# Attention scores as native float32 products of row halves, and another order of work in the staging of two weight matrices

## Chip, cores and metric

The kernel runs on one core of a Trainium2 chip. The metric is device microseconds of one execution, as the median of several runs.

## What is computed

Four batches of attention with 12 heads, 448 positions and head size 64, with a mix of the heads before and after the softmax; then two blocks of dense layers on the 1792 x 768 result. All inputs are float32, and the products keep about that precision.

```python
scores = scale * np.matmul(q, k.transpose(0, 1, 3, 2))
scores = np.einsum('bhij,hg->bgij', scores, w_pre)
attn = np.exp(scores - np.max(scores, axis=-1, keepdims=True))
attn = attn / (np.sum(attn, axis=-1, keepdims=True) + 1e-09)
attn = np.einsum('bhij,hg->bgij', attn, w_post)
x = np.matmul(attn, v)                     # to [1792, 768]
h = (x @ w1) * (x @ w2) @ w3
x = h @ w_out
h = np.maximum(x @ w_in, 0.0)
out = h * h @ w_out2
```

## The kernel before

Engines are named as the profile does: PE is TensorE, DVE VectorE, ACT ScalarE, POOL GpSimd, SP the queue that issues loads. Every engine runs its instructions in the order in which the program was written; that order is fixed by hand, by tables of steps.

**Staging of weights (class Weights, and Prod34, which uses it first).** Since `w3` and `w_out` are applied one after the other, the kernel first multiplies them with each other. A product of about float32 precision is made of three fast ones: each operand is split into a high part (rounded to the type float32r) and a low part (the difference), and `mm3` (L54) adds high x high, high x low and low x high. Weights arrive as 64-bit words, and a piece goes through: a load on SP (L69), `narrow` on ACT (L81), three joins of bits on DVE (L93, L95, L97) that give float32 `f`, `high` on ACT (L111), `rest`, the low part, on POOL (L115). `Prod34.half0` walks over 25 pieces: for each of eight chunks two of 384 columns (`wo`) and one of 512 (`w3`), and multiplies each chunk into eight accumulators, 24 products of 384 columns a chunk. `stage(s)` sets what is done ahead for later pieces: load 6 ahead, narrow 4, joins 3 and 2 (the joins of two pieces interleaved), high 2, rest 1. At its end ACT and DVE copy the accumulators out (L195, L196). `half1` does the same with eight more `w3` pieces: a loop over chunks with 12 products each, then four groups of 24 products.

**Prologue of attention.** `prologue(i)` is called after each chunk, with i from 0 to 7 in half0 and from 8 to 19 in half1. The table PRO says at which i the first chunk of queries (n = 0) is loaded, split and scored. From i = 15 on it also runs the first steps of attention.

**Attention.** Queries come in 16 chunks of 120 or 88 rows (four a batch), each cut into 12 or 9 blocks of up to 10 rows x 12 heads; there are 180 blocks g. Step g of `attention_step` issues for TensorE in this order: pv (L478, of an earlier chunk, in some steps), premix of block g + 1 (sp, L380), scores of a later chunk (sc, L358, in some steps), tmix of block g - 4 (tp, L436). Scores leave PSUM through ACT (`evac`, L365), are regrouped by a DMA (L372), mixed, and turned by rowmax (DVE), expo (ACT), a sum scaled on POOL, p_hi (ACT) and p_lo (DVE, L426) into half-precision high and low parts; after tmix, p2 (L449 on ACT, L451 on DVE) takes them out of PSUM.

**Scores before.** K has its 64 rows twice on the partitions of the loaded tile: rows 0 to 63 become the high part (a cast on ACT in the first batch, on DVE later: L312, L310), rows 64 to 127 the low part (L319). Q is doubled likewise and split into `qh` (L334, L336) and `ql` (L341). So one product over 128 rows gives q-part x (k high + k low), and a head is two products of 448 columns, `qh` and `ql`, into one of two PSUM banks. premix and pv use float32 operands as they are; the trace shows each such product as two records. pv writes its two heads to the PSUM partitions 0 to 63 and 64 to 127.

Of the kernel before, what the change touches and what calls it, by code (L numbers as in the profile page):

```python
# [34 lines left out]
def fused_kernel(ctx, tc, q, k, v, w_pre, w_post, w1, w2, w3t, wo, win, wo2, eye, out):  # L35
# [22 lines left out]
    class Weights:  # L58
# [60 lines left out]
    class Prod34:  # L119


        def __init__(self, p, stg, spare):
            self.p, self.stg, self.spare = p, stg, spare
            self.w = Weights(stg, PW, 5, 3, 4, 2, 2)
# [10 lines left out]
            for i in range(-6, 0):  # L135
                self.stage(i)

        def tile(self, k, c, x):
            if (k, c, x) not in self.t:
                n = HC if k == "o" else PW  # L140
                p = self.p if x else self.stg
                kw = {"tag": "w3{}", "bufs": 2} if (k, x) == ("3", 0) else {"tag": "w" + k + "{}" + f"{c}_{x}"}
                self.t[k, c, x] = tuple(
                    p.tile([128, n], R, name=f"w{k}{e}{c}_{x}", tag=kw["tag"].format(e), bufs=kw.get("bufs", 1))
                    for e in "hl"
                )
            return self.t[k, c, x]

        def stage(self, s):
            w = self.w  # L150
            ok = lambda i: 0 <= i < len(self.seq)
            if ok(s + 6):
                k, c, x, lo, hi, _ = self.seq[s + 6]
                src, n = (wo, HC) if k == "o" else (w3t, PW)
                w.load(s + 6, src[c, :, n * x + lo : n * x + hi], True)
            if ok(s + 4):
                w.narrow(s + 4)
            if ok(s + 2) and s > 0:
                w.join(s + 2, 1)
            if ok(s + 3):  # L160
                w.join(s + 3, 0)
                if s < 0:
                    w.join(s + 3, 1)
                    w.join(s + 3, 2)
            if ok(s + 2):
                if s >= 0:
                    if s == 0:
                        w.join(s + 2, 1)
                    w.join(s + 2, 2)
                k, c, x, lo, hi, _ = self.seq[s + 2]  # L170
                w.place(s + 2, tuple(t[:, lo:hi] for t in self.tile(k, c, x)))
                w.high(s + 2)
            if ok(s + 1):
                w.rest(s + 1)
# [6 lines left out]
        def half0(self, ps, between):  # L181
# [8 lines left out]
            for m in range(4):  # L190
                if m > 1:
                    self.stage(self.n0 - 2 + m)
                o = f32(self.spare.tile([128, 2, S], R, tag="kt", name=f"o34_{m}", bufs=8))
                o = o.rearrange("p e j -> p (e j)")[:, :DM]
# [6 lines left out]
        def store(self, m, h, acc):  # L201
            if m % 2 == 0:
                self.o = self.spare.tile([128, 3, 2, 128], F, tag="kraw", name=f"o34_{m}_{h}", bufs=2)
# [38 lines left out]
    class Attention:  # L242
        def __init__(self, const, ka, ps):
            self.const, self.ka, self.ps, self.sc = const, ka, ps, {}
            self.done = set()
            self.kt, self.kraw, self.qraw, self.qh, self.ql = {}, {}, {}, {}, {}
# [14 lines left out]
        def setup_load(self):  # L261
            nc.vector.memset(self.ones, 1.0)
            for x in self.phl:
                for t in x:
                    nc.vector.memset(t[:, S:], 0.0)
# [13 lines left out]
        def setup_post(self):  # L279
            kw, kab = (self.ka.tile([120, 12, 10], F, tag="qraw", name=x, bufs=2) for x in ("kw", "kab"))  # L280
# [17 lines left out]

        def load_k(self, b, r):
            if b == 0 and r in (2, 3):  # L300
                raw = f32(self.ka.tile([128, 2, S], R, tag="kt", name=f"kraw{b}_{r}", bufs=8))
            else:
                raw = self.ka.tile([128, 2, S], F, tag="kraw", name=f"kraw{b}_{r}", bufs=2)
            nc.sync.dma_start(raw, k[b, :, 2 * r : 2 * r + 2])
            self.kraw[b, r] = raw

        def high_k(self, b, r):
            t = self.ka.tile([128, 2, S], R, tag="kt", name=f"kt{b}_{r}", bufs=8)
            if b:
                nc.vector.tensor_copy(t, self.kraw[b, r])  # L310
            else:
                nc.scalar.activation(t, self.kraw[b, r], AF.Copy)  # L312
            self.kt[b, r] = t

        def low_k(self, b, r):
            raw, t = self.kraw.pop((b, r)), self.kt[b, r]
            for e in range(2):
                eng = nc.gpsimd if b else nc.vector
                eng.tensor_tensor(t[64:128, e], raw[64:128, e], f32(t[64:128, e]), ALU.subtract)  # L319
            self.done.add(("k", b, r))  # L320

        def load_q(self, n, g4):
            b, c = divmod(n, 4)
            i0, ic, _ = CHUNKS[c]
            o = 12 * i0 + 4 * g4 * ic
            raw = self.ka.tile([128, 4 * IC], F, tag="qraw", name=f"qraw{n}_{g4}", bufs=2)
            nc.sync.dma_start(raw[:, : 4 * ic], q[b, :, o : o + 4 * ic])
            self.qraw[n, g4] = raw[:, : 4 * ic]

        def high_q(self, n, g4):  # L330
            th = self.ka.tile([128, 4 * IC], R, tag="qh", name=f"qh{n}_{g4}", bufs=3)
            th = self.qh[n, g4] = th[:, : 4 * CHUNKS[n % 4][1]]
            if n:
                nc.vector.tensor_copy(th, self.qraw[n, g4])  # L334
            else:
                nc.scalar.activation(th, self.qraw[n, g4], AF.Copy)  # L336

        def low_q(self, n, g4):
            tl = self.ka.tile([128, 4 * IC], R, tag="ql", name=f"ql{n}_{g4}", bufs=3)
            tl = self.ql[n, g4] = tl[:, : 4 * CHUNKS[n % 4][1]]  # L340
            nc.gpsimd.tensor_tensor(tl, self.qraw.pop((n, g4)), f32(self.qh[n, g4]), ALU.subtract)  # L341

        def split_q(self, n, g4):
            self.high_q(n, g4)
            self.low_q(n, g4)

        def scores(self, n, h):
            b, c = divmod(n, 4)
            ic = CHUNKS[c][1]
            assert ("k", b, h // 2) in self.done  # L350
            if h == 0:
# [3 lines left out]
            sc = self.ps.tile([IC, S], F, tag="sc", name=f"sc{n}_{h}", bufs=2)  # L355
            g4, hh = divmod(h, 4)
# [4 lines left out]
            self.sc[n, h] = sc  # L361

        def evac(self, n, h):
            ic = CHUNKS[n % 4][1]
            nc.scalar.activation(self.st[n][:ic, h], self.sc.pop((n, h))[:ic], AF.Copy)  # L365
            self.done.add(("s", n, h))

        def regroup(self, g):
            n, r, nr, o, cnt = blocks[g]
            assert all(("s", n, h) in self.done for h in range(NH))  # L370
# [83 lines left out]
        def p2_act(self, g):  # L454
            if g % 4 == 0:
                self.p2_evac(g, 0)

        def p2_dve(self, g):
            if g % 4:
# [34 lines left out]
    def spread(lo, hi, items):  # L494
# [3 lines left out]
    AT = {"sc": 1, "lq": 6, "hq": 3, "pv": 5, "k": -9, "ks": 4, "v": -6}  # L498
# [6 lines left out]
        "load_q": (2, 4, 9), "split_q": (5, 8, 13), "load_k": (7, 7, 8, 8, 8, 8), "high_k": (8, 9, 9, 12, 12, 12),  # L505
        "low_k": (9, 10, 12, 13, 13, 13), "scores": (10, 11, 12, 13, 15, 14), "evac": (10, 11, 13, 14, 15, 14),
# [3 lines left out]
    def attention_plan():  # L510
# [5 lines left out]
        for n in range(16):  # L516
            b = n // 4
            if n:
                for t, h in spread(first[n - 1] - RG + AT["sc"], first[n] - RG - 1, range(NH)):
                    add(t, "scores", n, h)  # L520
# [389 lines left out]
```

## Time and profile before

| | us |
|---|---|
| median of 3 runs | 1403.97 (1403.86 to 1404.88) |
| the profiled execution | 1406.93 |
| its span, in which the rows are counted | 1405.1 |
| PE busy | 1360.5 (97%) |
| DVE busy | 919.4 (65%) |
| ACT busy | 714.0 (51%) |
| POOL busy | 413.5 (29%) |

The span has four parts: 0 to 66 us half0, 66 to 129.7 half1 with the first steps of attention, 129.7 to about 563 attention, and the dense layers to the end. A row of the timeline gives start, length and instruction; where PE's instructions overlap in its pipeline, the time of one is read from start to start. In the table of stages the figure behind the engines is the granted clock of PE as a share of 2.4 GHz.

### The profile page before, as it was taken

How to read it: one execution, taken by the hardware profiler on the slowest of the kernel's cores; microseconds unless marked ns; L12 is line 12 of the kernel's file. 1: busy time of each engine (PE TensorE's matmuls, PEld its weight loads, DVE VectorE, ACT ScalarE, POOL GpSimd, SP SyncE). 2: the span in 40 equal slices, each digit the busy share in tenths (PEclk: the TensorE clock that was granted, in tenths of full speed). 3: DMA queues.
4: the chain of work that ended last, by engine and by line, in shares of the span. 5: the costliest groups of instructions: out<-in, count | busy, mean ns of one | idle time of the engine just before them, and what ended most of it. 6: DMA issues, size and time to landing. Idle time of an engine off the chain costs nothing.

```text
span 1405.1 us, 24056 instructions
## 1 busy us (share of the span) xinstructions
PE 1360.5 (97%) x8858; PEld 1141.8 (81%) x8858; DVE 919.4 (65%) x1561; ACT 714.0 (51%) x1529; POOL 413.5 (29%) x424
## 2 busy tenths in 40 slices
PE   6779999999999998999999999999999999999998
PEld 5767666667667666899999999999999999999998
DVE  8963887886887779655217944985555128935962
ACT  4455887877777877434224533543343224533430
POOL 4531351351242113222222222233222222322231
PEclk9889999999999999999999999999999999999999
DMA  7754455454545335434123342455343123432341
GB/s 216 228 187 159 157 167 163 158 177 150 169 165 169 119 128 157 139 102 113 54 69 101 124 120 73 122 176 175 115 115 91 59 78 96 131 115 79 117 145 54
DMA packets 95514, 183.77 MB, mean 131 GB/s; under 512 B 20581, under 2 KB 62053, under 8 KB 94949
## 3 DMA queue, kind: packets, MB, share of 16 engines
q1 hardware_dynamic: 89861, 178.82, 41.2%
q10 hardware_dynamic: 5536, 3.42, 0.8%
q8 instruction: 70, 1.15, 0.4%
q14 instruction: 47, 0.39, 0.1%
HBM read 129.52 MB, written 14.16 MB: 102 GB/s over the span
## 4 chain that ended last, share of the span: by engine, by line
PE 89%; DVE 5%; ACT 2%; issue 2%; DMA 1%; POOL 1%; DVEq 0%; ACTq 0%; POOLq 0%
PE l L54 50%; PE sp L380 10%; PE y L54 8%; PE tp L436 7%; PE pv L478 6%; PE sc L358 5%; PE q L54 2%; DVE pl L426 1%; DVE f L93 1%; DVE f L95 1%; DVE f L97 1%; PE p L54 1%; DVE p L451 1%; PE e L54 1%; ACT ph L419 1%
## 5 line engine op out<-in xcount | busy, mean ns | idle before, releaser
L115 POOL TENSOR_TENSOR wl<-f,wh 128x384 fp32r<-128x384 f32 (+1 forms) x176 | 195.6, 1115 | 508.5 <-ACT wh L111 492.8
L93 DVE TENSOR_SCALAR f<-y 128x384 int32<-128x384 int32 (+2 forms) x209 | 146.9, 703 | 88.2 <-POOL wl L115 83.3
L426 DVE SCALAR_TENSOR_TENSOR pl<-p,sm,ph 120x448 f16<-120x448 f32 x180 | 138.9, 772 | 77.0 <-ACT ph L419 76.3
L380 PE MATMUL sp<-r,kpre 120*120 120x448 f32 x360 | 178.2, 577 | 1.2 <-ACT p L394 0.8
L436 PEld LDWEIGHTS <-ph 120*128 120x128 f16 (+1 forms) x1440 | 105.5, 98 | 52.6 <-issue 52.6
L97 DVE SCALAR_TENSOR_TENSOR f<-raw,f 128x384 int32<-128x384 int32 (+2 forms) x209 | 140.4, 672 | 6.1
L95 DVE SCALAR_TENSOR_TENSOR f<-y,f 128x384 int32<-128x384 int32 (+2 forms) x209 | 140.3, 672 | 6.1
L54 PE MATMUL l<-blh,wh 128*128 128x448 f32 x384 | 141.1, 368 | 0.0
L54 PE MATMUL l<-bhh,wl 128*128 128x448 f32 x384 | 141.1, 368 | 0.0
L54 PE MATMUL l<-bhh,wh 128*128 128x448 f32 x384 | 141.1, 368 | 0.0
L111 ACT ACTIVATE wh<-f 128x384 fp32r<-128x384 f32 (+1 forms) x176 | 96.5, 549 | 86.5 <-DVE f L97 80.9
L365 ACT ACTIVATE s<-sc 120x448 f32<-120x448 f32 (+1 forms) x192 | 99.2, 543 | 76.4 <-PE sc L358 73.0
L436 PE MATMUL tp<-kwh,ph 120*128 120x120 f16 x720 | 125.7, 219 | 1.1 <-DVE p L451 1.1
L394 ACT ACTIVATE p<-sp,nm 120x448 f32<-120x448 f32 x180 | 114.2, 635 | 23.4 <-DVE nm L386 21.9
L386 DVE TENSOR_REDUCE nm<-sp 120x1 f32<-120x448 f32 x180 | 110.6, 615 | 21.0 <-PE sp L380 19.8
L358 PE MATMUL sc<-kt,qh 128*120 128x448 f32 (+1 forms) x192 | 119.5, 622 | 5.0 <-DVE kt L319 4.6
L436 PE MATMUL tp<-kwh,pl 120*128 120x120 f16 x720 | 124.1, 216 | 0.0
L436 PE MATMUL tp<-kwl,ph 120*128 120x120 f16 x720 | 124.0, 216 | 0.0
L81 ACT ACTIVATE y<-raw 128x384 f32<-128x384 f32 (+2 forms) x209 | 120.6, 577 | 5.9 <-DMA raw<-w3t 3.8
L419 ACT ACTIVATE ph<-p,sm 120x448 f16<-120x448 f32 x180 | 119.9, 666 | 5.8 <-DVE sm L414 4.6
L478 PE MATMUL pv<-p,v 112*64 112x120 f32 (+1 forms) x1536 | 94.6, 266 | 6.5 <-DVE p L451 6.2
L409 POOL TENSOR_SCALAR sm<-sm 120x2 f32<-120x2 f32 (+3 forms) x94 | 25.9, 276 | 254.4 <-ACT p L394 226.5
(122 smaller groups left out, 3155.5 us busy)
## 6 DMA issues: line engine op xcount, KB each, us to landing
r<-s SPq DMA_DIRECT2D x172, 210.0 KB
raw<-w SPq DMA_DIRECT2D x64, 384.0 KB
raw<-win SPq DMA_DIRECT2D x64, 384.0 KB
raw<-wo SPq DMA_DIRECT2D x48, 512.0 KB
kraw<-k SPq DMA_DIRECT2D x24, 448.0 KB
qraw<-q SPq DMA_DIRECT2D x36, 240.0 KB
raw<-w3t SPq DMA_DIRECT2D x15, 512.0 KB
raw<-wo SPq DMA_DIRECT2D x16, 384.0 KB
```

The source lines that it names most:

```text
L54: nc.tensor.matmul(acc, w, x, start=(first and i == 0 and j == 0), stop=(last and i == n - 1 and j == 2))
L81: nc.scalar.activation(y, self.raw[i][:, :, 1].bitcast(F), AF.Copy, scale=2.0**-112)
L93: nc.vector.tensor_scalar(fi, yi, 3, 0x7FFFFFFF, ALU.logical_shift_left, ALU.bitwise_and)
L95: nc.vector.scalar_tensor_tensor(fi, yi, -0x80000000, fi, ALU.bitwise_and, ALU.bitwise_or)
L97: nc.vector.scalar_tensor_tensor(fi, raw[:, :, 0], 29, fi, ALU.logical_shift_right, ALU.bitwise_or)
L115: nc.gpsimd.tensor_tensor(self.out[i][1], self.ft.pop(i), f32(self.out[i][0]), ALU.subtract)
L358: nc.tensor.matmul(sc[:ic], t[:, hh * ic : hh * ic + ic], self.kt[b, h // 2][:, h % 2], start=(i == 0), stop=(i == 1))
L380: nc.tensor.matmul(t[:kk], self.kpre[:kk, :kk], self.rt.pop(g)[:kk], start=True, stop=True)
L419: nc.scalar.activation(self.phl[g % NP][0][:kk, :S], self.pt[g][:kk], AF.Copy, scale=self.sm[g // 2][:kk, g % 2 : g % 2 + 1])
L426: nc.vector.scalar_tensor_tensor(l, self.pt.pop(g)[:kk], self.sm[g // 2][:kk, g % 2 : g % 2 + 1], h, ALU.mult, ALU.subtract)
L436: nc.tensor.matmul(t[:, j, :, :cnt], p[:kk, j * JP : j * JP + 128], w[:kk, :, :cnt], start=(i == 0), stop=(i == 2))
L478: nc.tensor.matmul(t[64 * e : 64 * e + 64], self.v[b][:, j, g], self.p2[n][:, j, g, :ic], start=(j == 0), stop=(j == JC - 1),)
```

## The change

**Scores.** The host lays q and k out so that the even head of a pair has partitions 0 to 63 and the odd one 64 to 127, not doubled, half the bytes. They are used as loaded: all splits of q and k (L310 to L341) are gone, with their tiles. A pair of heads is four native float32 products over 64 rows of 224 columns, even and odd head in turn, into one tile of two PSUM banks, one bank a head; there is one such tile, where there were two of one bank. ACT evacuates both heads in one instruction. Of q one load a chunk replaces three, five steps ahead of the first scores; k comes as six tiles a batch, ten buffers. In the prologue scores of n = 0 are at i = 9 to 14, evacuations at 10 to 15.

**Staging of Prod34.** `stage(s)` now loads 8 ahead, narrows 6, joins 4 (all three of one piece together), high 3, rest 2; the low part is on DVE. Raw buffers are 6 instead of 5, those of the first half of `w3` 3 instead of 2.

**Also:** p2 is on ACT for every eighth block, not every fourth; the cleared edges of `ph` and `pl` are set on POOL; the tiles `o34`, `kw` and `kab` have a tag of their own; the two early heads of the dense layers share one tile.

```diff
-        def rest(self, i):
+        def rest(self, i, eng=nc.gpsimd):
             if i in self.ft:
-                nc.gpsimd.tensor_tensor(self.out[i][1], self.ft.pop(i), f32(self.out[i][0]), ALU.subtract)
+                eng.tensor_tensor(self.out[i][1], self.ft.pop(i), f32(self.out[i][0]), ALU.subtract)
...
-            for i in range(-6, 0):
+            for i in range(-8, 0):
                 self.stage(i)
...
+            if ok(s + 8):
+                k, c, x, lo, hi, _ = self.seq[s + 8]
+                src, n = (wo, HC) if k == "o" else (w3t, PW)
+                w.load(s + 8, src[c, :, n * x + lo : n * x + hi], True)
+            if ok(s + 3):
+                k, c, x, lo, hi, _ = self.seq[s + 3]
+                w.place(s + 3, tuple(t[:, lo:hi] for t in self.tile(k, c, x)))
+                w.high(s + 3)
             if ok(s + 6):
...
+                w.narrow(s + 6)
+            if ok(s + 2):
+                w.rest(s + 2, nc.vector)
             if ok(s + 4):
...
+                for part in range(3):
+                    w.join(s + 4, part)
...
-            for i, t in enumerate((self.qh[n, g4], self.ql[n, g4])):
-                nc.tensor.matmul(
-                    sc[:ic], t[:, hh * ic : hh * ic + ic], self.kt[b, h // 2][:, h % 2], start=(i == 0), stop=(i == 1)
-                )
...
+            sc = self.sc[n, x] = self.ps.tile([IC, 2, 512], F, tag="sc", name=f"sc{n}_{x}", bufs=1)
+            qt, kt = self.qt[n][:, x], self.kt[b, x]
+            for o in (0, S // 2):
+                w = slice(o, o + S // 2)
+                for e in range(2):
+                    h = slice(64 * e, 64 * e + 64)
+                    nc.tensor.matmul(sc[:ic, e, w], qt[h], kt[h, w], start=True, stop=True)
...
-            nc.scalar.activation(self.st[n][:ic, h], self.sc.pop((n, h))[:ic], AF.Copy)
...
+            nc.scalar.activation(self.st[n][:ic, 2 * x : 2 * x + 2], self.sc.pop((n, x))[:ic, :, :S], AF.Copy)
...
-            if g % 4 == 0:
+            if g % 8 == 0:
...
-    AT = {"sc": 1, "lq": 6, "hq": 3, "pv": 5, "k": -9, "ks": 4, "v": -6}
+    AT = {"sc": 1, "lq": 5, "pv": 5, "k": -6, "ks": 3, "v": -6}
...
-        "load_q": (2, 4, 9), "split_q": (5, 8, 13), "load_k": (7, 7, 8, 8, 8, 8), "high_k": (8, 9, 9, 12, 12, 12),
-        "low_k": (9, 10, 12, 13, 13, 13), "scores": (10, 11, 12, 13, 15, 14), "evac": (10, 11, 13, 14, 15, 14),
+        "load_q": (3,), "load_k": (4, 4, 5, 5, 6, 6), "scores": (9, 10, 11, 12, 13, 14), "evac": (10, 11, 12, 13, 14, 15),
         "pre": 2, "post": 12, "steps": (7, 1, 4, 2, 1),
```

On DVE, in half0 around piece 13 (the number behind `f`, `y` and `raw` is the piece's), there stands before:

```order
L93 TENSOR_SCALAR f13_344<-y13_313 128x384
L97 SCALAR_TENSOR_TENSOR f12_316<-raw12_251,f12_316 128x384
L95 SCALAR_TENSOR_TENSOR f13_344<-y13_313,f13_344 128x384
L93 TENSOR_SCALAR f14_356<-y14_341 128x512
L97 SCALAR_TENSOR_TENSOR f13_344<-raw13_275,f13_344 128x384
L95 SCALAR_TENSOR_TENSOR f14_356<-y14_341,f14_356 128x512
```

and in the changed kernel, on the same engine around the same pieces (`wol` and `w3l` are low parts):

```order
L115 TENSOR_TENSOR wol3_1_332<-f12_313,woh3_1_331 128x384
L93 TENSOR_SCALAR f14_363<-y14_310 128x512
L95 SCALAR_TENSOR_TENSOR f14_363<-y14_310,f14_363 128x512
L97 SCALAR_TENSOR_TENSOR f14_363<-raw14_269,f14_363 128x512
L115 TENSOR_TENSOR wol4_0_358<-f13_337,woh4_0_357 128x384
L93 TENSOR_SCALAR f15_375<-y15_334 128x384
L95 SCALAR_TENSOR_TENSOR f15_375<-y15_334,f15_375 128x384
L97 SCALAR_TENSOR_TENSOR f15_375<-raw15_293,f15_375 128x384
```

The joins of two pieces no longer alternate, and between two pieces stands the low part of the piece before last.

On PE, in an attention step with pv and scores (step 25, scores of chunk 3; `ph` is the stationary operand of tp), there stands before:

```order
L478 MATMUL pv0_3_1806<-p20_1225,v0_949 64x120 x8
L380 MATMUL sp26_1892<-r26_1731,kpre_115 120x448
L358 MATMUL sc3_6_1894<-kt0_3_835,qh3_1_1721 88x448
L358 MATMUL sc3_6_1894<-kt0_3_835,ql3_1_1766 88x448
L358 MATMUL sc3_7_1897<-kt0_3_835,qh3_1_1721 88x448
L358 MATMUL sc3_7_1897<-kt0_3_835,ql3_1_1766 88x448
L436 LDWEIGHTS ph0_119
L436 MATMUL tp21_1900<-kwh_117,ph0_119 128x120
```

and in the changed kernel, in the same step on the same engine:

```order
L432 MATMUL pv0_3_1673<-p20_1144,v0_895 64x120 x8
L334 MATMUL sp26_1749<-r26_1600,kpre_129 120x448
L315 MATMUL sc3_3_1751<-kt0_3_543,q3_1414 88x224 x4
L390 LDWEIGHTS ph0_133
L390 MATMUL tp21_1756<-kwh_131,ph0_133 128x120
```

The place in the step is the same; four products of 448 columns over 128 rows became four of 224 columns over 64 rows, in native float32 (the order shows one row for both records of such a product).

## Rows read from the trace of the kernel before

**Rows 1.** Stages: busy us of PE, PEld, DVE, ACT, POOL; clock, DMA share, GB/s.
```profile
0.00:66.00 66.00, 45.44 (x192) 40.76 (x192) 60.80 (x93) 30.96 (x59) 34.32 (x31) 0.90 0.72 215
66.00:104.00 38.00, 27.88 (x123) 24.93 (x124) 28.24 (x44) 19.99 (x36) 15.25 (x11) 0.82 0.63 199
...
129.70:537.00 407.30, 402.84 (x4019) 279.20 (x4019) 325.31 (x610) 322.06 (x746) 120.47 (x167) 1.00 0.48 158
...
66.00:80.00 14.00, 9.02 (x41) 7.74 (x42) 13.94 (x18) 9.54 (x16) 7.18 (x6) 0.88 0.97 323
```

**Rows 2.** Timeline of TensorE, three attention steps (start, length in us, instruction).
```profile
269.88 0.23 PE L436 MATMUL tp<-kwh,ph 120*128 120x120 f16 x1
...
270.52 0.97 PE L380 MATMUL sp<-r,kpre 120*120 120x448 f32 x2
271.33 0.22 PE L436 MATMUL tp<-kwh,ph 120*128 120x120 f16 x1
...
272.05 1.04 PE L478 MATMUL pv<-p,v 112*64 112x120 f32 x16
273.02 1.01 PE L380 MATMUL sp<-r,kpre 120*120 120x448 f32 x2
273.87 0.21 PE L436 MATMUL tp<-kwh,ph 120*128 120x120 f16 x1
...
276.13 0.23 PE L436 MATMUL tp<-kwh,ph 120*128 120x120 f16 x1
```

**Rows 3.** Groups of instructions from 129.7 to 537 us: scores on TensorE.
```profile
L358 PE MATMUL sc<-kt,qh 128*120 128x448 f32 x121 | 76.4, 632 | 0.0
...
L358 PE MATMUL sc<-kt,qh 128*88 128x448 f32 x48 | 31.6, 658 | 0.0
```

**Rows 4.** Timeline of VectorE and GpSimd while weights are staged.
```profile
20.78 0.68 DVE L95 SCALAR_TENSOR_TENSOR f<-y,f 128x512 int32<-128x512 int32 x1
...
21.50 1.11 POOL L115 TENSOR_TENSOR wol<-f,woh 128x384 fp32r<-128x384 f32 x1 [1.39 <-ACT woh L111]
...
21.66 1.50 DVE L97 SCALAR_TENSOR_TENSOR f<-raw,f 128x512 int32<-128x512 int32 x1
...
23.08 0.55 DVE L95 SCALAR_TENSOR_TENSOR f<-y,f 128x384 int32<-128x384 int32 x1
...
23.55 0.35 DVE L93 TENSOR_SCALAR f<-y 128x384 int32<-128x384 int32 x1
...
32.90 0.41 DVE L93 TENSOR_SCALAR f<-y 128x512 int32<-128x512 int32 x1
...
37.29 0.35 DVE L93 TENSOR_SCALAR f<-y 128x384 int32<-128x384 int32 x1
```

**Rows 5.** Groups by form: VectorE's float32 subtractions elsewhere in the kernel.
```profile
L699 DVE TENSOR_TENSOR blh<-h,bhh 128x448 fp32r<-128x448 f32 x64 | 39.5, 617 | 0.0
...
L688 DVE TENSOR_TENSOR x1l<-x1l,x1h 128x720 fp32r<-128x720 f32 x4 | 3.6, 901 | 0.0
```

**Rows 6.** Timeline of VectorE: first join, and first copy out of the accumulators.
```profile
4.69 0.29 DVE L93 TENSOR_SCALAR f<-y 128x256 int32<-128x256 int32 x1 [4.69 <-ACT y L81]
...
65.19 1.01 DVE L196 COPY o<-p 128x384 f32<-128x384 f32 x2
```

**Rows 7.** Waits from 66 to 104 us (us in total, times, longest).
```profile
PE pc L287 <- DVE kab L285: 4.7, 1, 4.7
PE sc L358 <- DVE kt L319: 4.6, 2, 4.2
DVE kab L285 <- POOL ql L341: 4.2, 1, 4.2
```

**Rows 8.** The chain that ended last, near 104 us (start, us, what).
```profile
104.16 4.17 PE q L54 x24
```

**Rows 9.** Timeline of TensorE: a pv group of 88 columns.
```profile
253.41 0.83 PE L478 MATMUL pv<-p,v 112*64 112x88 f32 x16
254.17 1.01 PE L380 MATMUL sp<-r,kpre 120*120 120x448 f32 x2
```

More of the change, by code (lines that the diff above doesn't have):

```diff
@@ L279, in setup_post @@
         def setup_post(self):
-            kw, kab = (self.ka.tile([120, 12, 10], F, tag="qraw", name=x, bufs=2) for x in ("kw", "kab"))
+            kw, kab = (self.ka.tile([120, 12, 10], F, tag="o34", name=x, bufs=4) for x in ("kw", "kab"))
             nc.vector.tensor_tensor(
@@ L299, in load_k @@
         def load_k(self, b, r):
[L300 to L322, printed above, removed]
+            t = self.kt[b, r] = self.ka.tile([128, S], F, tag="kt", name=f"kt{b}_{r}", bufs=10)
+            nc.sync.dma_start(t, k[b, :, r])
+        def load_q(self, n):
@@ L338, in low_q @@
[L338 to L347, printed above, removed]
+            t = self.ka.tile([128, 6 * IC], F, tag="q", name=f"q{n}", bufs=2)
+            self.qt[n] = t[:, : 6 * ic].rearrange("p (r i) -> p r i", i=ic)
@@ L348, in scores @@
+            nc.sync.dma_start(t[:, : 6 * ic], q[b, :, 6 * i0 : 6 * (i0 + ic)])
+        def scores(self, n, x):
             b, c = divmod(n, 4)
             ic = CHUNKS[c][1]
-            assert ("k", b, h // 2) in self.done
-            if h == 0:
+            if x == 0:
                 self.st[n] = (self.ka if n % 2 == 0 else self.kc).tile(
@@ L518, in attention_plan @@
             if n:
-                for t, h in spread(first[n - 1] - RG + AT["sc"], first[n] - RG - 1, range(NH)):
-                    add(t, "scores", n, h)
-                    if h % 4 == 0:
-                        add(t - AT["lq"], "load_q", n, h // 4)
-                        add(t - AT["hq"], "high_q", n, h // 4)
+                for t, x in spread(first[n - 1] - RG + AT["sc"], first[n] - RG - 1, range(NH // 2)):
+                    add(t, "scores", n, x)
+                add(first[n - 1] - RG + AT["sc"] - AT["lq"], "load_q", n)
             for t, x in spread(first[n + 1] + AT["pv"], first[n + 2] + AT["pv"], range(NH // 2)):
@@ L527, in attention_plan @@
             for r in range(NH // 2):
-                t = first[4 * b - 2] + AT["k"] + AT["ks"] * r
-                add(t - 3, "load_k", b, r)
-                add(t, "high_k", b, r)
+                add(first[4 * b - 2] + AT["k"] + AT["ks"] * r, "load_k", b, r)
         for b in range(B):
@@ L801, in prologue @@
                 A.setup_pre()
[L802 to L804 removed]
+            for x in at("load_k"):
+                A.load_k(0, x)
+            for x in at("load_q"):
+                A.load_q(x)
             for x in at("evac"):
[L806 to L811 removed]
+                A.evac(0, x)
             for x in at("scores"):
[L813 to L816 removed]
+                A.scores(0, x)
             if i == PRO["post"]:
@@ L841, in fused_kernel @@
                 tail = M.tail_plan()
-                heads = (x for i in range(2) for x in M.early(
-                    i, lambda i: ps.tile([128, TB], F, tag="sc", name=f"e{i}", bufs=2)
-                ))
+                pair = ps.tile([128, 2, 512], F, tag="sc", name="e", bufs=1)
+                heads = (x for i in range(2) for x in M.early(i, lambda i: pair[:, i, :TB]))
             u = g - closed - 1
@@ L882 @@
     qt = q.transpose(0, 3, 1, 2)
-    qt = np.concatenate([qt[..., o].reshape(B, D, -1) for o in order], axis=2)
-    kt = k.transpose(0, 3, 1, 2)
+    qt = np.concatenate(
+        [qt[..., o].reshape(B, D, 6, 2, -1).transpose(0, 3, 1, 2, 4).reshape(B, 128, -1) for o in order], axis=2
+    )
+    kt = k.reshape(B, 6, 2, S, D).transpose(0, 2, 4, 1, 3).reshape(B, 128, 6, S)
     def words(w):
```

79 lines of the change are left out of this document (15 added, 64 removed).

## Prediction

> **What bounds the kernel now.** I read the busy times by stage first, then the order of TensorE's instructions inside one attention step, then the two stages before it. Attention, from 129.7 to 537 us, is 407 us long and TensorE is busy for 402.8 of them, while VectorE and ScalarE have 325 and 322 us [rows 1]. That this busy time is real work shows in the single steps: a step with transpose-mix (tp) and premix (sp) alone takes 271.33 - 269.88 = 1.45 us, one with a pv group 273.87 - 271.33 = 2.54, one with two heads of scores 276.13 - 273.87 = 2.26 [rows 2], and the other steps of their kinds repeat these times. So in this stage whatever a pair of heads costs TensorE is paid in full: a pair now costs 2.26 - 1.45 = 0.81 us. The stage holds 121 + 48 = 169 heads of scores [rows 3], that is 84.5 pairs; 5.5 pairs stand in the four last weight products before it, and 6 in the loop before those.
>
> The first 104 us are different. From 0 to 66 us VectorE is busy for 60.8 of 66, TensorE for 45.4, at a granted clock of 0.90; from 66 to 104 TensorE has 27.9 of 38 at 0.82 [rows 1].
>
> **Change, part one: the staging of the first 66 us.** VectorE sets the pace here: two chunks last from 23.55 to 37.29, 6.87 us each [rows 4]. Undisturbed, the joins of a 384-wide piece cost 0.35 + 2 x 0.55 = 1.45 us and those of a 512-wide one 0.41 + 2 x 0.68 = 1.77 [rows 4], so a chunk (two narrow pieces, one wide) needs 4.67; the rest of the 6.87 is lost beside GpSimd, as in the 1.50 us of the join at 21.66, which has a low part of GpSimd's at its side from 21.50 on, against 0.68 for the same shape undisturbed [rows 4]. The change gives VectorE the low parts. The nearest rows are its subtractions of 448 and 720 float32 columns, 0.617 and 0.901 us [rows 5], 1.04 ns a column: 0.55 us for 384 and 0.68 for 512. A chunk then costs 2 x (1.45 + 0.55) + 1.77 + 0.68 = 6.45 us and GpSimd is idle, so nothing stretches it. That is 0.4 us a chunk, 3 us in all. But these 3 us do not come out at the end: the pieces of the next stage are staged deeper ahead, and the two copies that free the accumulators stand behind them in VectorE's queue. Joins begin at 4.69 [rows 6]; eight chunks (51.6), four wide joins ahead (7.1), two wide low parts (1.4) put the first copy at about 64.8, against 65.19 now [rows 6]. ScalarE, busy for 31 of the 66 us [rows 1], hides its share. The loads come two pieces earlier and the k loads stand between them on SP's queue; the transfers moved 323 GB/s from 66 to 80 us [rows 1], and the 1.3 MB of a chunk plus 0.45 MB of k in 6.45 us ask for some 270.
>
> **Part two: the loop from 66 to 104 us.** Its own TensorE work is 96 products of 4.17/24 = 0.174 us [rows 8] and six pairs, 16.7 + 6 x 0.81 = 21.6 us; it lasts 38. The rest is waiting and the low clock that follows it: TensorE waits 4.6 us for a split k and 4.7 for kab, which itself waited 4.2 for GpSimd's split of q, because it takes over that tile's buffer [rows 7]. All of these go, since k and q are used as they land, and kab takes its buffer from stores that are long done. What is late next is TensorE itself: VectorE has only four low parts and two joins left there. From 64.8: 16.7 + 6 x 1.06 (part three) + 0.8 for the small product of setup_post = 88.7, against 104.16 now [rows 8], 15.5 us earlier; I keep half a microsecond for low clock: **-15 us**. It is -10 if the clock stays low for half of the loop, -18 if the first stage also ends earlier. v and the second q stand ahead of the first regroup on SP's queue, 1.7 MB, 5.3 us at that rate; they go out when staging ends near 77, and are first wanted near 93.
>
> **Part three: what a pair costs in native float32.** No row shows row halves. The nearest are the pv groups, native float32 in column halves: eight products that the trace shows as 16 records, in 0.97 us for 120 columns (272.05 to 273.02) [rows 2] and 0.76 for 88 (253.41 to 254.17) [rows 9]. Thirty-two columns more cost 0.21 us, 6.6 ns a column for 16 records, 0.41 for one; a premix, two records of 448 columns alone on the array, takes 0.81 us, 0.90 ns a column [rows 2]. So two halves run at the same time. What does not scale is larger: a pv step costs 2.54 - 1.45 = 1.09 us, of which 120 x 6.6 ns = 0.79 is columns and 0.30 is not: entering the group, loading its first weights, leaving it.
>
> The change makes eight records of 224 columns from a pair, four slots of 224 x 0.82 ns = 0.74 us in all. With the 0.30 of a pv group, and 0.02 for a first weight load of 120 columns instead of 64, a pair costs **1.06 us** instead of 0.81: +0.25. The bounds are 0.76 (nothing to enter or leave) and 8 x 0.184 + 0.32 = 1.79 (halves one after the other). I take 1.06, since pv is the one row with tiles of this type. On 84.5 + 5.5 = 90 pairs this is **+22.5 us**; the six of the loop are in part two already.
>
> The 0.30 us that pv pays beyond its columns has a rule on the Trainium skill's page TensorEngine Tiling (Array Packing), Key Properties: changing the tiling mode, not just the tile, drains TensorE. By that rule each pair pays two such changes, between premix and scores and between scores and tp, and the sum is the one above; a pair that paid neither would come out near 0.76, and the change would be a gain (rival 1). The pv rows agree with the rule for column halves; no row shows it for row halves.
>
> **Small terms.** The casts of q and k leave VectorE and the low parts leave GpSimd; TensorE's idle time in attention is 407.3 - 402.8 = 4.5 us [rows 1], and some of it is waiting for p, whose steps on VectorE stretch beside GpSimd; I take **-3** (0 to -5). One evacuation of a pair replaces two, and every eighth instead of every fourth tp goes to ScalarE, so VectorE gets about 22 more over attention, under its slack of 82 us there [rows 1]; near its end, where it also joins weights, I take **+0.5**. The single score buffer makes the next pair wait for one long evacuation, with a tp and a premix, 1.45 us, between them: nothing.
>
> **Sum.** -15 + 22.5 - 3 + 0.5 = +5 us on the profiled execution's span of 1405.1. That execution took 1406.9 in all, 3 above the median of 1403.97; the difference is carried to the median: **1409 us**.
>
> **Rivals.** (1) *Entering and leaving row halves is free or cheap.* A pair costs 0.76 to 0.92, so 90 pairs move by -4.5 to +10 us and the loop gains 1 to 2 more: -24 to -8 us in sum, 1380 to 1396. For it: a weight load may start under the running premix, which the 0.30 of pv does not have ahead of it. Against: pv pays on both of its sides. The change turns faster once a pair costs less than about 1.00. (2) *The halves do not pair.* If the second half starts one pass later, five slots instead of four, or if the weight loads of the halves go one after the other, a pair costs 1.15 to 1.3 and the total is 1418 to 1432; wholly serial, at 1.79, 96 x 0.73 = 70 us more than forecast, near 1479. Against it: pv pairs without a lost slot. (3) *The staging does not deliver.* If the loads cannot keep 270 GB/s or low clock takes half of the loop, part two gives 8 instead of 15: 1416.
>
> **How the numbers follow.** The forecast has 0.53; its own bounds (part two -18 to -12, a pair 1.01 to 1.10, the small terms) give 1399 to 1418, so of the 0.53 some 0.07 is faster by over 0.2% (about what a measurement of this kernel can tell from no change), 0.16 within 0.2%, 0.30 slower. Rival 1 has 0.25, all faster; rival 2 0.12 and rival 3 0.10, slower. Faster 0.32, same 0.16, slower 0.52. The range leaves out two fifths of rival 1 and half of rival 2: 1387 to 1423.
>
> **What would show it.** Right: the first of the four 24-fold weight products starts near 89 us; steps of attention keep one time per kind, with 1.45 and 2.54 unchanged and those with scores at 2.51; VectorE's joins in the first stage all take their undisturbed time. Rival 1 shows steps with scores at 2.2 to 2.4, rival 2 above 2.6, rival 3 TensorE waiting in the loop on y or w3. The forecast is wrong as a whole if attention steps of one kind no longer repeat, for then another engine has become the bound.

## The result: 0.7% slower, and where the 9 microseconds come from

| | before | changed |
|---|---|---|
| median, us | 1403.91 (4 runs) | 1413.34 (4 runs) |
| ratio | | 1.007, 95% interval 1.0053 to 1.0088 |
| profiled span, us | 1405.1 | 1412.3 |
| first tmix of attention, us | 129.68 | 125.30 |
| first to last tmix, us | 430.1 | 444.6 |
| last tmix to the end of the span, us | 845.3 | 842.4 |

So the time grew by 9.4 us: the start gained 4.4 and attention lost 14.5. The last part is code that the change hardly touches (two early heads share a tile). It ran 0.3% faster in this execution, on TensorE that is never idle from 750 to 1100 us, in the changed kernel and not in the kernel before; the run *fixed* below, with the same code there as the changed kernel, has the pace of before (the rows: TensorE's busy time and products in the same 350 us of before, after and *fixed*).

```profile
750.00:1100.00 350.00, 350.00 (x1698) 317.66 (x1697) 221.56 (x362) 141.45 (x284) 102.35 (x91) 1.00 0.40 120
...
750.00:1100.00 350.00, 350.00 (x1704) 319.99 (x1703) 226.68 (x369) 141.86 (x285) 101.48 (x90) 1.00 0.41 121
...
750.00:1100.00 350.00, 350.00 (x1697) 317.50 (x1697) 223.60 (x364) 141.91 (x287) 101.36 (x90) 1.00 0.41 120
```

That leaves 7.2 us on the span; with the last part set equal it is 14.5 - 4.4 = 10.1, near the 9.4 of the medians. The times of one kernel hold executions of both paces, so a difference below 0.2% says little by itself; below, places in the trace decide. Those of the start scatter too: *whole*, *inturn* and *pv_scores* below, which change nothing at the start that costs more or less by itself, have their first tmix at 124.1 to 124.9.

**Attention.** The table of stages, columns as in [rows 1], from first to last tmix: first before, then after.

```profile
129.70:559.80 430.10, 422.79 (x4276) 294.09 (x4276) 346.91 (x648) 340.23 (x785) 129.75 (x176) 1.00 0.48 157
...
125.30:569.90 444.60, 439.97 (x4611) 291.94 (x4609) 318.63 (x609) 324.33 (x675) 27.89 (x98) 1.00 0.39 131
```

TensorE works 17.2 us more and idles 4.6 us instead of 7.3. The timeline of TensorE after, to be held against [rows 2], shows the kinds of steps (start, length, instruction):

```profile
183.60 0.22 PE L390 MATMUL tp<-kwh,ph 120*128 120x120 f16 x1
...
185.04 0.22 PE L390 MATMUL tp<-kwh,ph 120*128 120x120 f16 x1
...
187.58 0.22 PE L390 MATMUL tp<-kwh,ph 120*128 120x120 f16 x1
...
188.21 0.97 PE L334 MATMUL sp<-r,kpre 120*120 120x448 f32 x2
189.11 1.02 PE L315 MATMUL sc<-kt,q 64*120 64x224 f32 x8
190.06 0.23 PE L390 MATMUL tp<-kwh,ph 120*128 120x120 f16 x1
```

tp and sp alone: 1.44. With pv: 2.54. With a pair of scores: 2.48, so the pair costs 1.04 (1.02 with 88 queries). Before, two heads in one step cost 0.81 to 0.83, and one head alone, as in 95 of the 132 steps with scores, 0.42: a pair cost 0.83 on average. The premix ahead of it runs 0.90 us to the next start instead of the 0.80 it takes before a tp, and the eight records take 0.95. Nearly all steps of one kind repeat these times through the whole stage.

**First stage.** VectorE after, start of one chunk's wide piece to that of the next:

```profile
20.12 0.42 DVE L93 TENSOR_SCALAR f<-y 128x512 int32<-128x512 int32 x1
...
22.38 0.35 DVE L93 TENSOR_SCALAR f<-y 128x384 int32<-128x384 int32 x1
...
23.36 0.56 DVE L97 SCALAR_TENSOR_TENSOR f<-raw,f 128x384 int32<-128x384 int32 x1
23.84 0.68 DVE L115 TENSOR_TENSOR w3l<-f,w3h 128x512 fp32r<-128x512 f32 x1
...
26.36 0.42 DVE L93 TENSOR_SCALAR f<-y 128x512 int32<-128x512 int32 x1
...
64.89 1.01 DVE L187 COPY o<-p 128x384 f32<-128x384 f32 x2
```

Every join takes its undisturbed time, a chunk 6.24 us instead of 6.87 [rows 4] (6.67 without two small operations that fell into those rows), and VectorE never stops; the first copy stands at 64.89 (65.19 before, [rows 6]).

**The loop of half1.** Its 24-fold products start at 96.99, 7.0 us earlier than the 103.99 of the timeline before (the chain of [rows 8] has 104.16, where the product ahead ends). Of the waits of [rows 7] none is left, but others stand there. Waits after, from 64 to 97 us; TensorE's timeline, the first line from before, the others from after; ScalarE's timeline after; and the chain that ended last, after:

```profile
ACT w3h L111 <- DVE f L97: 3.1, 2, 1.8
...
PE sc L315 <- ACT s L319: 3.2, 1, 3.2
PE q L54 <- ACT o L186: 2.6, 2, 2.4
```

```profile
103.99 0.34 PE L54 MATMUL q<-woh,w3h 128*128 128x384 f32 x1
...
74.37 0.34 PE L54 MATMUL q<-woh,w3l 128*128 128x384 f32 x1
77.92 1.85 PE L315 MATMUL sc<-kt,q 64*120 64x224 f32 x8 [3.21 <-ACT s L319]
79.70 0.69 PE L54 MATMUL q<-woh,w3h 128*128 128x384 f32 x1
80.18 0.52 PE L54 MATMUL q<-wol,w3h 128*128 128x384 f32 x1
80.50 0.52 PE L54 MATMUL q<-woh,w3l 128*128 128x384 f32 x1
...
96.99 0.34 PE L54 MATMUL q<-woh,w3h 128*128 128x384 f32 x1
```

```profile
74.04 0.63 ACT L111 ACTIVATE w3h<-f 128x512 fp32r<-128x512 f32 x1 [1.30 <-DVE f L97]
76.43 0.63 ACT L111 ACTIVATE w3h<-f 128x512 fp32r<-128x512 f32 x1 [1.76 <-DVE f L97]
76.97 0.90 ACT L319 ACTIVATE s<-sc 120x896 f32<-120x896 f32 x1
```

```profile
70.46 0.69 DVE f L97
...
75.71 0.70 DVE f L97
76.43 0.63 ACT w3h L111
77.06 0.81 ACT s L319
77.92 1.85 PE sc L315 x8
```

The second pair needs the one score tile, which waits for its evacuation; that stands on ScalarE behind the high parts of later weight pieces, which wait for the last joins on VectorE. TensorE stands still for 3.2 us, and then runs its products at 0.32 us from start to start (80.18 to 80.50) instead of 0.174 until 83.8: the granted clock of 80 to 88 us is 0.75, with the lower of the two levels (1.2 of 2.4 GHz) at its start. *whole*, *inturn* and *pv_scores*, whose tables for the loop are the same, have this wait as well, 2.4 to 4.1 us long; there the 24-fold products start at 95.7 to 96.2.

### The profile page after: what moved, and what is told of

Read it like the earlier page. It is cut to its first block, busy times and chain, and to the rows that moved or that the text cites. A ratio compares the mean times of both kernels' runs of the same rounds, so it can differ in the third digit from the quotient of the medians.

```text
span 1412.3 us, 24358 instructions
## 1 busy us (share of the span) xinstructions
PE 1374.8 (97%) x9242; PEld 1137.1 (81%) x9242; DVE 874.0 (62%) x1535; ACT 692.7 (49%) x1402; POOL 261.6 (19%) x313
## 4 chain that ended last, share of the span: by engine, by line
PE 90%; DVE 7%; ACT 1%; DMA 1%; issue 1%; SPq 0%; ACTq 0%
PE l L54 49%; PE sp L334 10%; PE y L54 8%; PE tp L390 7%; PE sc L315 6%; PE pv L432 6%; PE q L54 2%; DVE f L95 2%; DVE f L97 1%; DVE pl L380 1%; DVE f L93 1%; DVE p L405 1%; DVE w3l L115 1%; DMA x0l<-xd 1%; DVE wol L115 1%
## 5 line engine op out<-in xcount | busy, mean ns | idle before, releaser
L380 DVE SCALAR_TENSOR_TENSOR pl<-p,sm,ph 120x448 f16<-120x448 f32 x180 | 125.6, 698 | 119.0 <-ACT ph L373 119.0
L93 DVE TENSOR_SCALAR f<-y 128x384 int32<-128x384 int32 (+2 forms) x209 | 137.9, 660 | 88.0 <-POOL wl L115 82.4
L390 PEld LDWEIGHTS <-ph 120*128 120x128 f16 (+1 forms) x1440 | 109.5, 98 | 69.3 <-issue 69.3
L95 DVE SCALAR_TENSOR_TENSOR f<-y,f 128x384 int32<-128x384 int32 (+2 forms) x209 | 131.0, 627 | 7.1
L97 DVE SCALAR_TENSOR_TENSOR f<-raw,f 128x384 int32<-128x384 int32 (+2 forms) x209 | 130.2, 623 | 7.1
L319 ACT ACTIVATE s<-sc 120x896 f32<-120x896 f32 (+1 forms) x96 | 88.0, 916 | 94.1 <-PE sc L315 92.9
L363 POOL TENSOR_SCALAR sm<-sm 120x2 f32<-120x2 f32 (+3 forms) x94 | 19.7, 209 | 528.0 <-ACT p L348 527.8
L315 PEld LDWEIGHTS sc<-kt,q 64*120 64x120 f32 (+1 forms) x768 | 61.4, 174 | 65.6 <-issue 28.9
L405 DVE TENSOR_SCALAR p<-tp,iv 112x480 f32<-112x480 f32 (+1 forms) x157 | 110.3, 703 | 0.0
```

What stands on the lines that cost most here:

```text
L93: nc.vector.tensor_scalar(fi, yi, 3, 0x7FFFFFFF, ALU.logical_shift_left, ALU.bitwise_and)
L95: nc.vector.scalar_tensor_tensor(fi, yi, -0x80000000, fi, ALU.bitwise_and, ALU.bitwise_or)
L97: nc.vector.scalar_tensor_tensor(fi, raw[:, :, 0], 29, fi, ALU.logical_shift_right, ALU.bitwise_or)
L315: nc.tensor.matmul(sc[:ic, e, w], qt[h], kt[h, w], start=True, stop=True)
L380: nc.vector.scalar_tensor_tensor(l, self.pt.pop(g)[:kk], self.sm[g // 2][:kk, g % 2 : g % 2 + 1], h, ALU.mult, ALU.subtract)
L390: nc.tensor.matmul(t[:, j, :, :cnt], p[:kk, j * JP : j * JP + 128], w[:kk, :, :cnt], start=(i == 0), stop=(i == 2))
```

## Experiments

Each run is the changed kernel with one edit, but where it says otherwise. A time without a ratio is that of a single execution; a ratio is to the kernel before on the same chip.

**What a pair consists of: *twice*.**

```diff
-            for o in (0, S // 2):
+            for o in (0, S // 2, 0, S // 2):
```

> The four products of each pair are issued twice in a row into the same tile; nothing else changes, and the output stays the same. This separates columns from entering and leaving. My theory: four more slots of 0.19 us and no second entry, so a pair costs 1.78 us (1.75 to 1.82), some 0.75 more, and the time is near 1485 for 96 pairs. Rival: what a pair pays beyond its columns is paid per product, so that doubling doubles all: 2.06 us a pair, time near 1512.

Measured: 1481.75 us. TensorE's timeline:

```profile
273.06 1.78 PE L315 MATMUL sc<-kt,q 64*120 64x224 f32 x16
274.77 0.23 PE L390 MATMUL tp<-kwh,ph 120*128 120x120 f16 x1
```

Sixteen records take 1.71 us to the tp, eight took 0.95: +0.76, four slots of 0.19, in every step. So 0.76 of a pair are columns and 0.28 are paid once a group, close to what the prediction had (0.74 and 0.32).

**Whether fewer products are cheaper: *whole*.**

```diff
-            for o in (0, S // 2):
-                w = slice(o, o + S // 2)
-                for e in range(2):
-                    h = slice(64 * e, 64 * e + 64)
-                    nc.tensor.matmul(sc[:ic, e, w], qt[h], kt[h, w], start=True, stop=True)
+            for e in range(2):
+                h = slice(64 * e, 64 * e + 64)
+                nc.tensor.matmul(sc[:ic, e, :S], qt[h], kt[h], start=True, stop=True)
```

> Each head's product covers all 448 columns, so a pair is two products instead of four, with the same columns. If a pair costs four slots of columns (0.19 us each for 224) plus a fixed price for entering and leaving row halves, which is my theory, it stays at 1.03 us (1.00 to 1.06) and the time at 1413. If part of each slot is a price per product, the pair falls below 0.98 and the time below 1409. If the second half starts only behind the first record of the first, a pair pays half a product more: 1.2 us or above, and the time is near 1430.

Measured: 1412.63 us, steps with scores unchanged at 2.48. No price per product shows.

**What lets the halves run together: *inturn* and *onehalf*.**

```diff
-            for o in (0, S // 2):
-                w = slice(o, o + S // 2)
-                for e in range(2):
-                    h = slice(64 * e, 64 * e + 64)
+            for e in range(2):
+                h = slice(64 * e, 64 * e + 64)
+                for o in (0, S // 2):
+                    w = slice(o, o + S // 2)
```

> The same four products of a pair, but both of the even head first, then both of the odd one. If neighbours in the instruction order must be in different row halves to run at the same time, which is my theory, the eight records take seven or eight slots of 0.19 us instead of four: a pair costs 1.6 to 1.8 us, and with 96 pairs the time is 1468 to 1485. If TensorE pairs the halves by itself whatever the order, a pair stays at 1.03 and the time at 1413.

Measured: 1416.5 us, with the slower pace in the dense layers; a pair costs 1.04. My theory fell: the order does not matter. That left two readings, and *onehalf*, which leaves out the odd heads, tells them apart:

```diff
-                    h = slice(64 * e, 64 * e + 64)
+                    h = slice(0, 64)
```

> All four products of a pair read the even head's rows, 0 to 63, and write the same places as before; the odd head's scores are left out and replaced by the even head's. In the run named inturn a pair cost 1.04 us although neighbours in the order were in the same half, and the records don't say which half they are in. My theory by now: TensorE has one order for each row half and runs the next record of either half as soon as its rows are free, so with all eight records in one half they need eight slots, a pair costs 1.78 us, and the time is 1482 to 1486. Rival: what runs at the same time are the two records of one product, whichever rows they use; then a pair stays at 1.03 us and the time at 1413.

Measured: 1483.86 us. TensorE's timelines, *inturn* (88 queries) and *onehalf* (120):

```profile
273.71 1.00 PE L315 MATMUL sc<-kt,q 64*88 64x224 f32 x8
274.64 0.23 PE L390 MATMUL tp<-kwh,ph 120*128 120x120 f16 x1
```

```profile
274.06 1.77 PE L315 MATMUL sc<-kt,q 64*120 64x224 f32 x8
275.77 0.23 PE L390 MATMUL tp<-kwh,ph 120*128 120x120 f16 x1
```

Eight records in one half take 1.71 us, eight slots of 0.19 and the price of the group; in two halves 0.93 (0.95 with 120 queries), whichever way they are ordered. Read one by one, the records of *inturn* start in twos, 0.01 us apart. So records of the odd half start ahead of records of the even half that come before them in the program: TensorE starts them as their half becomes free. A record does not name its half, so the order is that of the kernel's text; a step between text and chip that changed it would look the same, and no run rules that out.

**What entering and leaving cost: *pv_scores*.**

```diff
-        ("pv", "premix", "scores", "tmix"),
+        ("pv", "scores", "premix", "tmix"),
```

> The changed kernel with the scores of a step between pv and premix instead of between premix and tmix. In the 42 or so steps that have both, TensorE then goes from column halves straight to row halves. My theory: of the 0.28 us that a pair costs beyond its columns, each change of tiling is a third, so a step with both falls from 3.59 to 3.45 to 3.50, a step with scores alone stays at 2.46, and the time is 4 to 6 us below the changed kernel's 1413. Rival: what is paid is for each kind of tiling that is entered, and a step with both stays at 3.59 and the time at 1413.

Measured: 1407.9 us; from first to last tmix 439.1 us instead of 444.6. Two steps of TensorE's timeline, with 88 queries:

```profile
270.01 0.22 PE L390 MATMUL tp<-kwh,ph 120*128 120x120 f16 x1
...
270.73 0.99 PE L315 MATMUL sc<-kt,q 64*88 64x224 f32 x8
271.66 1.01 PE L334 MATMUL sp<-r,kpre 120*120 120x448 f32 x2
272.51 0.22 PE L390 MATMUL tp<-kwh,ph 120*128 120x120 f16 x1
...
273.23 1.04 PE L432 MATMUL pv<-p,v 112*64 112x120 f32 x16
274.20 0.99 PE L315 MATMUL sc<-kt,q 64*88 64x224 f32 x8
275.12 1.01 PE L334 MATMUL sp<-r,kpre 120*120 120x448 f32 x2
275.97 0.22 PE L390 MATMUL tp<-kwh,ph 120*128 120x120 f16 x1
```

A step with both takes 3.46 here (3.48 at 120 queries, against 3.59): one change of tiling of four is gone. A step with scores alone rises from 2.48 to 2.52, for a reason that stays open. That is 42 x 0.11 - 42 x 0.04 = 2.9 of the 5.5 us; TensorE's idle time fell by 1.5, and 1.1 is not accounted for. If the 0.04 is paid in steps with both as well, one change costs 0.15 and not 0.11. The Trainium skill (TensorEngine Tiling (Array Packing), Key Properties) says that a change of the tiling mode drains TensorE. The 0.11 us saved with one change agrees with it; a drain as such is not seen in the trace.

**Which part does what: *staging_only* and *scores_only*.** The kernel before with the new `stage()` alone (buffers raised, three joined pieces), and the changed kernel with the old one. The core of the first edit; the second is the same turned round:

```diff
-            for i in range(-6, 0):
+            for i in range(-8, 0):
...
-            if ok(s + 1):
-                w.rest(s + 1)
+            if ok(s + 2):
+                w.rest(s + 2, nc.vector)
+            if ok(s + 4):
+                for part in range(3):
+                    w.join(s + 4, part)
```

> The kernel before with the staging of the changed kernel alone (the three raised buffer counts too, but three joined pieces instead of four, for space); scores, splits of q and k and the prologue's table stay as before. My theory: the waits of TensorE in the loop of the second stage, 4.6 us for a split k and 4.7 for kab, come from the splits and not from the staging, so the 24-fold products still start within 4 us of 104, an attention pair stays at 0.82 us, and the time is 1401 (1398 to 1404). Rival: the staging alone gives the 7 us by which the 24-fold products came earlier, and the time is near 1397 or below.

> The changed kernel with the order of staging of the kernel before (joins of two pieces interleaved, low parts on GpSimd, loads six pieces ahead). My theory: pairs in attention cost 1.03 us as in the changed kernel, 17 us more than before in sum, and the loop saves part of what it waited for split k and q, so the time is 1416 (1412 to 1421). Rival: the staging brought no part of the 7 us, and the time is 1413, as in the changed kernel.

Measured: *staging_only* 1403.19, ratio 0.9974 (0.9961 to 0.9986), most of which looks like pace, since its first tmix comes only 1.1 us earlier and its attention is 1.4 longer; *scores_only* 1416.23, ratio 1.007 (1.0052 to 1.0088). Waits of *staging_only* from 62 to 104 us:

```profile
DVE kab L277 <- POOL ql L333: 7.3, 1, 7.3
...
PE sc L350 <- DVE kt L311: 4.9, 1, 4.9
```

The staging alone brings the first tmix forward by 1.1 us (128.60), as the waits for the splits stay; the new scores alone by 1.7 (128.01), where TensorE waits 7.7 us for the first evacuation of scores. Both together gave 4.4. The first expectation held; of *scores_only* the time was as expected, and the 2.7 us that the staging adds in the trace (128.01 to 125.30) are about what the interval can hide. Differences of 1 us at this place are no more than the scatter named above.

**Where the loop's gain went: *later* and *fixed*.** *later* moves the scores and evacuations of the first chunk (where both stand at one i, the evacuation is written behind its scores):

```diff
-"scores": (9, 10, 11, 12, 13, 14), "evac": (10, 11, 12, 13, 14, 15),
+"scores": (11, 12, 13, 14, 15, 15), "evac": (12, 13, 14, 15, 15, 15),
```

> The six pairs of scores of the first chunk of queries come two chunks of weights later in the loop of the second staging stage (the last two together at its end), so that ScalarE has all high parts of the weights behind it before its first evacuation of scores. My theory of where the missing 8 us of the loop went: the first evacuation stands in ScalarE's queue behind high parts that wait for VectorE's joins, TensorE waits 3.2 us for the one score tile, and runs slower for some us after that. Then this wait goes, the 24-fold products start near 92 (90 to 94) instead of 97, and the time is 4 to 6 us below that of the changed kernel, near 1408.5. Rival: TensorE then reaches the last weight pieces before VectorE has joined them and waits there instead: they start at 95 to 97, and the time is within 2 us of 1413.

Measured: 1412.35, ratio 1.0057 (1.0036 to 1.0079). The wait at 74 us is gone and the clock is 1.00 from 64 to 88; the 24-fold products start at 93.95, as expected, but two pairs at the loop's end now stand behind the copies of the accumulators on ScalarE, the clock falls there (0.68 from 88 to 96), and the first tmix comes only 1.2 us earlier. The wait went as expected; the time (1408.5 expected) did not come, since the edit made new waits of 3.9 us. *fixed* keeps the first pair, moves the others by one chunk, and writes each evacuation right behind its scores:

```diff
-"scores": (9, 10, 11, 12, 13, 14), "evac": (10, 11, 12, 13, 14, 15),
+"scores": (9, 11, 12, 13, 14, 15), "evac": (9, 11, 12, 13, 14, 15),
...
+            for x in at("scores"):
+                A.scores(0, x)
             for x in at("evac"):
                 A.evac(0, x)
-            for x in at("scores"):
-                A.scores(0, x)
```

> The changed kernel with each evacuation of the first chunk's scores written right behind its scores, and pairs 1 to 5 one chunk later in the loop than in the changed kernel, pair 0 where it was. The two evacuations that can meet ScalarE's high parts then stand ahead of the last high part or behind it with no score waiting. The run before this one showed TensorE at a clock of 1.00 from 64 to 88 us with later scores, and lost it again at the loop's end, where two pairs stood behind the copies of the accumulators. My theory: here the 24-fold products start at 89 to 91 instead of 97, and the time is 6 to 8 us below the changed kernel's, 1405 to 1408. Rival: what is saved in the loop comes back as waiting for the first blocks of attention, and the time stays at 1411 to 1413.

Measured: 1408.59, a little outside the expected 1405 to 1408; ratio 1.0011 (0.9998 to 1.0024), where the changed kernel has 1.007. ScalarE's timeline, and two stretches of the table of stages, after and then *fixed*:

```profile
74.11 0.63 ACT L111 ACTIVATE w3h<-f 128x512 fp32r<-128x512 f32 x1 [1.30 <-DVE f L97]
74.65 0.90 ACT L319 ACTIVATE s<-sc 120x896 f32<-120x896 f32 x1
76.50 0.63 ACT L111 ACTIVATE w3h<-f 128x512 fp32r<-128x512 f32 x1 [0.95 <-DVE f L97]
```

```profile
72.00:80.00 8.00, 4.79 (x27) 3.53 (x24) 5.97 (x12) 2.88 (x5) 0.00 (x0) 0.82 0.55 146
80.00:88.00 8.00, 8.00 (x40) 6.84 (x39) 0.00 (x0) 1.66 (x2) 0.00 (x0) 0.75 0.46 126
...
72.00:80.00 8.00, 8.00 (x52) 7.14 (x50) 6.04 (x12) 3.60 (x5) 0.00 (x0) 1.00 0.52 136
80.00:88.00 8.00, 8.00 (x52) 6.71 (x49) 1.58 (x8) 2.81 (x4) 0.00 (x0) 1.00 0.51 136
```

The first evacuation goes out between two high parts, TensorE is never idle from 72 to 88 us, and the 24-fold products start at 90.2 us, the first tmix at 118.6, 6.7 us earlier than in the changed kernel. So the wait came from where the evacuation stands on ScalarE. How much of the gain is the evacuation's earlier place and how much the second pair's later one, *fixed* does not tell, since it changes both.

**A version that beats both: *mixed*.** Kernel before with the new staging; the scores of the first batch native in row halves (two products of 448 columns a pair, q and k as loaded, places as in *fixed*), the other three batches split as before. Its core:

```diff
+            if b == 0:
+                for e in range(2):
+                    self.sc[n, 2 * h + e] = self.ps.tile([IC, S], F, tag="sc", name=f"sc{n}_{2 * h + e}", bufs=2)
+                qt, kt = self.qn[n, h // 4][:, h % 4], f32(self.kt[b, h // 2])[:, h % 2]
+                for e in range(2):
+                    p = slice(64 * e, 64 * e + 64)
+                    nc.tensor.matmul(self.sc[n, 2 * h + e][:ic], qt[p], kt[p], start=True, stop=True)
+                return
```

*fixed_pv* is *fixed* with the order of *pv_scores*.

> What the runs so far point to: native float32 in row halves for the scores of the first batch alone (no split of q and k stands in the loop of the staging, with the places of scores and evacuations of the run named fixed), and the split scores of the kernel before, at 0.82 us a pair, for the three other batches; staging as in the changed kernel. My theory: the loop is as short as in fixed, so the first tmix of attention comes 11 us earlier than in the kernel before, the 12 to 13 native pairs behind it cost 0.2 us more each, 2.5 us, and the time is 8 to 9 us below the kernel before, 1395 (1392 to 1398). Rival: the staging of k for the second batch or something else of attention was tuned to the old start, waits appear there, and the time is 1399 or above.

> The run named fixed with scores between pv and premix: both corrections of the changed kernel together, all scores in native float32. My theory: the two gains are in different places, the loop (7 us of first tmix) and attention (5.4 us from first to last tmix), and add up: 10 to 12 us below the changed kernel, 1400 to 1403, level with the kernel before or up to 0.3% faster. Rival: they share something, and the time stays at 1405 or above.

Measured: *mixed* 1393.98 (ratio 0.9917, 0.9899 to 0.9935), as expected; *fixed_pv* 1403.2 (0.9983, 0.9971 to 0.9996), at the upper edge of what was expected and level with the kernel before, whose lowest time is 0.7 us above its own. *mixed*, loop and attention in the table of stages:

```profile
72.00:80.00 8.00, 8.00 (x41) 6.07 (x40) 5.70 (x12) 3.88 (x9) 0.00 (x0) 1.00 0.60 165
...
117.50:549.80 432.30, 425.48 (x4274) 290.28 (x4272) 343.38 (x642) 339.74 (x782) 123.14 (x170) 1.00 0.47 154
```

Its first tmix stands at 117.5, 12.2 us before that of the kernel before, and its attention is 2.2 us longer, 10.0 us in all: no split of q and k stands in the loop, and the dear pairs are few.

## Why the prediction was right, point by point

The forecast was 1409 with a sum of +5 us; measured are +9.4, inside the range, in the case that had the highest chance. That the number came so near is in part luck: the start fell short by 9 us, and attention and the pace of the last part gave some of it back.

- **Part one held, with two errors that cancel.** A chunk costs 6.24 us (forecast 6.45: subtractions and joins overlap a little from one to the next), 1.7 less over eight chunks; joins begin at 5.55 instead of 4.69, and small operations stand between them. So the first copy is at 64.89 (64.8).
- **Part two is the mis-sized term: -7.0 instead of -15** at the 24-fold products (96.99 against 88.7 + 0.5). Three sentences failed. "VectorE has only four low parts and two joins left there" leaves out the two pieces that are staged between the copies: behind the first copy at 64.89 stand four joins and six low parts, until 77.7, and the chain above runs through these joins. "The single score buffer ... nothing" was worked out for attention only; in the loop the evacuation's place on ScalarE's queue, behind high parts that wait for VectorE, decides. And "ScalarE ... hides its share" goes by a busy share of the first stage, while of the loop the prediction says nothing of ScalarE: it is busy for 11 of the 33 us there and still late. What stands in the gap, from rows: the start 0.6 earlier; waits for copies 0.7; low clock from 67 to 70 us, ten steps of 0.32 instead of 0.174, 1.5; the wait for the tile 3.4; low clock from 78 to 83.8, 2.6 (a pair at 1.78 instead of 0.95, twelve products at 0.32); six pairs at 1.14 with the restart of the products behind them, instead of 1.06, 0.5. Sum 8.1, for the 8.3 between 88.7 and 97. *fixed* shows nearly the forecast's loop: 90.2. Rival 3 had the size (8 instead of 15) and half of the cause: low clock took 4.1 of these 8 us, but no wait for `y` or a load is in the loop.
- **From the 24-fold products to the first tmix** the changed kernel takes 28.3 us, 2.6 more than before, where the forecast had 5.5 pairs at 0.25, 1.4. Six pairs stand there now instead of five and a half, and where products follow a pair the first takes 0.1 longer, as in the loop.
- **Part three held:** a pair costs 1.03 instead of the forecast 1.06, 1.02 with 88 queries and 1.04 with 120, with 0.76 for columns and 0.28 for the group (*twice*); the 0.02 that the forecast added for a longer first weight load is seen in no run by itself. Against 0.83 before, not 0.81, 84 pairs cost 17 us; TensorE's busy time in attention grew by 17.2. The borrowed 0.30 of pv was a good stand-in. Rivals 1 and 2 fell: steps with scores at 2.48, not at 2.2 to 2.4 or above 2.6.
- **Small terms:** idle time of TensorE in attention fell by 2.7 us (forecast 3); so first to last tmix is +14.5, where the forecast had 84.5 x 0.25 - 3 = 18. The +0.5 at the end can't be seen beside the pace of the dense layers.
- **The sum again, on the span:** -4.4 up to the first tmix (forecast -13.6: -15 and 5.5 pairs), +14.5 (18), -2.9 (+0.5; nearly all of it pace): +7.2, and 10.1 without the last part.

## What to carry to other kernels

When a change takes a wait away, look up what stands ahead of the next needed instruction on its own engine's queue: a small evacuation behind casts that wait for a full engine cost 3.4 us, and the low clock behind it 2.6 more. A group of products in another tiling of the array has a price that is paid once a group, here 0.28 us against 0.76 us of work, of which 0.11 went with one change of tiling; so bring such groups together or keep them to the place where their other gain is (here the first batch). And a price borrowed from the nearest rows (pv for scores) is good enough to decide, if the number of columns and of groups is kept apart.

## What the runs showed of the hardware

- Native float32 products in two row halves of the array run at the same time whatever their order: four records of one half, issued ahead of four of the other, cost as much as in turn (0.93 and 0.93 us for 88 queries), where eight in one half take 1.71 (120 queries). If the order of the kernel's text is that on the chip, TensorE starts products out of the program's order across halves, and the sentence ahead of the prediction that every engine keeps the written order doesn't hold for them. I had expected 1.6 us or more.
- Going straight from column halves to row halves, without a premix between them, saved 0.11 us a step, with one change of tiling less.
- The dense layers run at two paces some 0.3% apart: from the last tmix to the end nine of the thirteen traces take 842.0 to 842.6 us and four 845.3 to 845.5, at a granted clock of 1.00 and without idle time of TensorE from 750 to 1100 us. Each kernel has one trace; that one kernel shows both paces is read from its times (*mixed*: four from 1393.4 to 1394.3, two at 1397.5). The cause is open.
